# Rotary embedding of the first two pairs summed inside TensorE

## The chip, the cores and the metric

The kernel runs on one core of a Trainium2 chip. The core has TensorE (PE; its weight loads are listed apart as PEld), VectorE (DVE), ScalarE (ACT), GpSimd (POOL) and SyncE (SP, which issues most DMAs). PE reads SBUF and writes PSUM; the other engines move data between the two. The metric is the device time of one execution in microseconds (us), where less is better.

## What is computed

For 4 batches of 8 heads, 576 positions and head size 64, `q` and `k` are rotated (rotary embedding), softmax attention is taken, and the result goes through a mixer over positions and one over channels. In the reference:

```python
def rotate(x):
    x1, x2 = (x[..., :half], x[..., half:])
    return np.concatenate([x1 * cos - x2 * sin, x1 * sin + x2 * cos], axis=-1)
q_rot, k_rot = (rotate(q), rotate(k))
scores = scale * np.matmul(q_rot, k_rot.transpose(0, 1, 3, 2))
attn = softmax(scores); x = attn @ v
...
u = x + mix_over_positions(x);  out = u + relu(u @ w_ch1) @ w_ch2
```

## The kernel before

The 32 heads are worked on as 16 *pairs* (two heads of one batch, `n` = 0 to 15). The 576 positions are laid out as four rows `r` of 128 partitions and a fifth row of 64, kept in both partition halves, so a pair's `q` or `k` is a tile of 128 partitions x 5 rows x 2 heads x 64.

`prep(n)` loads `k`, `q` and `v` of a pair (`kraw`, `qraw`, `vraw`) and rotates `k` and `q` in three elementwise operations: `w = x * sin` (L486), `u = x * cos` (L488), and `u = u + w` with the two 32-wide halves of `w` exchanged (L492). Then TensorE transposes `u` in blocks of 64 partitions x 128 columns (L522, one instruction for each row `r` and partition half `z`), and ACT or DVE copies the result from PSUM to `kt` and `qt` (L540). For pair 0 the work is cut into rows 0 to 1 and rows 2 to 4, so that it starts before everything is loaded; I call these k part 1, k part 2 and so on. There is one `uk`, one `uq` and there are two `w` tiles, so pair 1 must wait for these tiles.

`pair(n)` makes scores (L666, 64 rows x 128 columns of weights, 288 columns moving; L584 for the fifth rows), scales them and takes the maximum on DVE (L551), the exponential on ACT (L563), transposes the probabilities on TensorE (L692, L608), copies them (L702), multiplies by `v` (L715), and normalizes (L744 and after). `warm` (L425) issues plain products with the identity into unused PSUM columns at the start, in which TensorE has nothing else to do. After the attention come the position mixer (L910, L932) and the channel mixer (L1001 to L1056).

All of it is fp32. A product that the code writes once is two pairs of records in the trace, a load of weights (LDWEIGHTS) and a product (MATMUL) each; a transpose is one pair. Blocks of 64 partitions use one half of TensorE's rows, so two of them (`z` = 0 and 1) can be under way at once.

What runs in which order is written out in two tables of numbers, `ORDER1` (1666 tasks, the attention and the first batch's position mixer) and `ORDER2` (195 tasks, the other position mixers and transposes). Each number is a task times four plus the chosen engine. PSUM banks are given out in this order too. Every engine then works through its own list in order. The later part of the channel mixer is ordered by the planner `Plan.run`.

Of the kernel before, what the change touches and what calls it, by code (L numbers as in the profile page):

```python
# [13 lines left out]
ALU = mybir.AluOpType  # L14
# [72 lines left out]
class Plan:  # L87
# [259 lines left out]
def rope_attention_mixer_kernel(ctx: ExitStack, tc: tile.TileContext, q, k, v, w_tok1, w_tok2, w_ch1, w_ch2, tab, out):  # L347
# [8 lines left out]
    nc = tc.nc  # L356
# [29 lines left out]
    def attention(ctx):  # L386
# [50 lines left out]
        def none(deps, bufs):  # L437
            return add("DVE", 0.0, None, deps, bufs)
# [5 lines left out]
        def prep(n):  # L444
# [3 lines left out]
            for nm, src, pr in (("k", k, 0.0), ("q", q, 0.5), ("v", v, 1.0)):  # L448
# [51 lines left out]
                for r0, r1 in parts:  # L500
                    if r0:
                        x = x + l[1:]
# [650 lines left out]
```

## Time and profile before

| what | us |
|---|---|
| three runs, median (lowest to highest) | 592.54 (592.42 to 592.59) |
| the profiled execution | 592.55 |
| its span, first to last instruction | 590.8 |
| PE busy in the span | 584.0 |
| DVE, ACT, POOL busy | 382.9, 312.9, 297.9 |

The profile lists the busy time of each engine, the share that it is of the span, and the chain of work that ended last: from the last instruction back to what released it, step by step. A busy PE isn't PE at its peak, since records of products contain a fixed latency and overlap; the pace is read from the distance between the starts of many like instructions. The granted clock of TensorE is full in the records of all stretches.

### The profile page before, as it was taken

How to read it: one execution, taken by the hardware profiler on the slowest of the kernel's cores; microseconds unless marked ns; L12 is line 12 of the kernel's file. 1: busy time of each engine (PE TensorE's matmuls, PEld its weight loads, DVE VectorE, ACT ScalarE, POOL GpSimd, SP SyncE). 2: the span in 40 equal slices, each digit the busy share in tenths (PEclk: the TensorE clock that was granted, in tenths of full speed). 3: DMA queues.
4: the chain of work that ended last, by engine and by line, in shares of the span. 5: the costliest groups of instructions: out<-in, count | busy, mean ns of one | idle time of the engine just before them, and what ended most of it. 6: DMA issues, size and time to landing. Idle time of an engine off the chain costs nothing.

```text
span 590.8 us, 12857 instructions
## 1 busy us (share of the span) xinstructions
PE 584.0 (99%) x4897; PEld 463.1 (78%) x4897; DVE 382.9 (65%) x1123; ACT 312.9 (53%) x797; POOL 297.9 (50%) x255
## 2 busy tenths in 40 slices
PE   8999999999999999999999999999999999999997
PEld 7767677777777676787888888888888888888886
DVE  6999989989999996789776543345423443222332
ACT  4999999999999998454444431333203311010110
POOL 4998498869779332323766761477404750000000
PEclk9999999999999999999999999999999999999999
DMA  5444122234141101022222220222102100001123
GB/s 141 140 133 131 33 69 68 74 79 147 38 141 27 32 1 55 7 85 72 53 63 68 64 75 1 70 65 53 28 0 72 37 1 0 1 0 72 71 72 107
DMA packets 34094, 36.15 MB, mean 61 GB/s; under 512 B 13809, under 2 KB 27633, under 8 KB 34033
## 3 DMA queue, kind: packets, MB, share of 16 engines
q1 hardware_dynamic: 32640, 34.81, 20.3%
q8 instruction: 38, 0.62, 0.4%
q10 hardware_dynamic: 1392, 0.52, 0.3%
q14 instruction: 24, 0.19, 0.1%
HBM read 30.61 MB, written 4.72 MB: 60 GB/s over the span
## 4 chain that ended last, share of the span: by engine, by line
PE 97%; DVE 2%; DMA 1%; ACT 0%; issue 0%; POOL 0%; DVEq 0%
PE s L1027 25%; PE s L1054 25%; PE s L715 14%; PE s L666 11%; PE s L692 7%; PE s L932 5%; PE s L910 4%; PE s L522 2%; PE s L584 2%; PE s L608 1%; PE s L1001 1%; PE s L744 1%; DVE p L551 1%; DMA tabs<-in_tab_dram 1%; DVE uq L492 0%
## 5 line engine op out<-in xcount | busy, mean ns | idle before, releaser
L1029 ACT ACTIVATE gh<-s 128x512 fp32r<-128x512 f32 (+1 forms) x60 | 33.3, 556 | 178.5 <-PE s L1027 178.5
L563 ACT ACTIVATE p<-p,nm 128x576 f32<-128x576 f32 x128 | 98.9, 778 | 2.5 <-DVE p L551 2.1
L1031 DVE SCALAR_TENSOR_TENSOR gl<-s,gh 128x512 fp32r<-128x512 f32 (+1 forms) x60 | 38.3, 638 | 95.2 <-ACT gh L1029 95.2
L1027 PE MATMUL s<-uh,c1h 128*128 128x512 f32 (+1 forms) x240 | 88.6, 369 | 0.0
L1027 PE MATMUL s<-ul,c1h 128*128 128x512 f32 (+1 forms) x240 | 88.3, 368 | 0.0
L1027 PE MATMUL s<-uh,c1l 128*128 128x512 f32 (+1 forms) x240 | 88.3, 368 | 0.0
L1056 DVE TENSOR_TENSOR X<-s,X 128x512 f32<-128x512 f32 (+1 forms) x65 | 44.4, 684 | 67.7 <-PE s L1054 67.5
L1054 PE MATMUL s<-c2l,gh 128*128 128x512 f32 (+1 forms) x219 | 84.6, 386 | 0.0
L1054 PE MATMUL s<-c2h,gh 128*128 128x512 f32 (+1 forms) x219 | 84.6, 386 | 0.0
L1054 PE MATMUL s<-c2h,gl 128*128 128x512 f32 (+1 forms) x219 | 84.5, 386 | 0.0
L715 PE MATMUL s<-pt,vraw 128*64 128x256 f32 (+1 forms) x640 | 84.5, 411 | 0.0
L666 PE MATMUL s<-kt,qt 64*128 64x288 f32 x512 | 78.1, 419 | 0.3 <-ACT kt L540 0.3
L715 PEld LDWEIGHTS s<-pt,vraw 128*64 128x64 f32 x640 | 43.7, 136 | 29.6 <-DVE p L551 1.3
L702 ACT COPY pt<-s 128x256 f32<-128x256 f32 (+1 forms) x167 | 59.6, 408 | 6.3 <-PE s L692 5.0
L551 DVE TENSOR_SCALAR_CACHE_REDUCE p<-s,nm 128x288 f32<-128x288 f32 x128 | 61.7, 512 | 1.8
L812 POOL TENSOR_TENSOR fa<-fc,fa 128x512 f32<-128x512 f32 (+3 forms) x31 | 34.8, 1123 | 52.2 <-DVE fa L810 27.3
L692 PEld LDWEIGHTS s<-ident,p 64*128 64x128 f32 x1152 | 46.1, 139 | 15.9 <-ACT p L563 3.9
L551 DVE TENSOR_SCALAR_CACHE_REDUCE p<-s 128x288 f32<-128x288 f32 x128 | 54.4, 452 | 2.5 <-PE s L666 1.8
L666 PEld LDWEIGHTS s<-kt,qt 64*128 64x128 f32 x512 | 49.9, 187 | 6.8 <-DVE p L551 0.9
L692 PE MATMUL s<-ident,p 64*128 64x64 f32 x1152 | 51.6, 226 | 0.3
L1027 PEld LDWEIGHTS s<-uh,c1h 128*128 128x128 f32 x240 | 45.2, 188 | 7.7
L1027 PEld LDWEIGHTS s<-ul,c1h 128*128 128x128 f32 x240 | 45.2, 188 | 7.6
(117 smaller groups left out, 1062.7 us busy)
## 6 DMA issues: line engine op xcount, KB each, us to landing
stg<-in_moe_w_ch_dram SPq DMA_DIRECT2D x16, 384.0 KB, 3.2
stg<-in_moe_w_ch_dram SPq DMA_DIRECT2D x12, 512.0 KB, 3.6
vraw<-in_v_dram SPq DMA_DIRECT2D x16, 256.0 KB, 3.0
kraw<-in_k_dram SPq DMA_DIRECT2D x15, 256.0 KB, 3.3
qraw<-in_q_dram SPq DMA_DIRECT2D x15, 256.0 KB, 3.4
out_dram<-X SPq DMA_DIRECT2D x15, 256.0 KB, 2.3
stg<-in_moe_w_tok_dram SPq DMA_DIRECT2D x4, 512.0 KB, 4.2
kraw<-in_k_dram SPq DMA_DIRECT2D x32, 32.0 KB, 2.6
```

The lines of the kernel that those rows point to most:

```text
L551: return lambda: nc.vector.tensor_scalar(out=p()[:, c * W2:(c + 1) * W2], in0=sb.t[:, 0:W2], scalar1=-D ** -0.5, scalar2=nm.t[:, 0:1] if c ...
L563: return lambda: nc.scalar.activation(out=p(), in_=p(), func=ACTF.Exp, bias=nm.t[:, 1:2], scale=-1.0, accum_out=l())
L666: nc.tensor.matmul(sbs[h].t[:, c0:c0 + W2], flat(qt.t)[halves[h], TL + j * P:TL + (j + 1) * P], flat(kt.t)[halves[h], TL * (1 - h) + u * W ...
L692: nc.tensor.transpose(xy[z].t[:, i * TL:(i + 1) * TL], pb.t[halves[z], c0:c0 + P], ident[halves[z], halves[z]])
L702: return lambda: e(out=pt[c].t[:, R * h:R * h + m, o + z * TL:o + (z + 1) * TL], in_=xy[z].t[:, 0:m * TL].rearrange("p (r s) -> p r s", r=m))
L715: nc.tensor.matmul(ab.t[halves[h], 0:w], vb.t[:, h, r, :], m, start=(r == 0), stop=(r == R))
L812: mul_ = lambda e: lambda: e.tensor_tensor(out=A(), in0=C(), in1=A(), op=ALU.mult)
L1027: nc.tensor.matmul(tb.t[:, 0:n], a, m, start=(i == 0), stop=(i == len(lst) - 1))
L1029: x = add("ACT", act(n), lambda f=f, tb=tb: nc.scalar.activation(out=gb.t[0][:, f, 0:n], in_=tb.t[:, 0:n], func=ACTF.Relu), [x], [tb, gb], ...
L1031: y = add("DVE", dve(n), lambda f=f, tb=tb: nc.vector.scalar_tensor_tensor(out=gb.t[1][:, f, 0:n], in0=tb.t[:, 0:n], scalar=0.0, in1=gb.t[ ...
L1054: nc.tensor.matmul(tb.t[:, 0:w], a, m, start=(i == 0), stop=(i == len(lst) - 1))
L1056: y = add("DVE", dve(w) + 0.08, lambda u=u, tb=tb, cols=cols, w=w: nc.vector.tensor_tensor(out=u[:, cols], in0=tb.t[:, 0:w], in1=u[:, cols ...
```

## The change

For the first two pairs (`n < ADDED`, with `ADDED = 2`) the third elementwise operation, the addition, is left out. The first operation writes `w` with its two halves already exchanged. In place of one transpose of `u`, TensorE makes two plain products with the identity into the same PSUM place, one of `u` and one of `w`, the second added to the first. The two elementwise operations no longer stand one behind the other (each waits for the load alone), and `w` is held until TensorE has read it. Pairs 2 to 15 are as before. Both order tables are new throughout.

```diff
 ORDER1 = (
-    72, 68, 80, 84, 88, 92, 96, 104, 100, 0, 12, 16, 21, 24, 4, 28, 32, 8, 40, 44, 48, 52, 76, 60, 108, 112, 152, 156, 148, 184, 56, 161, 36, 64, 1408,
...
+        ADDED = 2
...
-                        if i == 0:
+                        if i == 0 and n < ADDED:
+                            turn = lambda x: x.rearrange("p r h (a j) -> p r h a j", a=2)
+                            e.tensor_tensor(out=turn(w)[:, :, :, ::-1], in0=turn(src), in1=turn(bc(1)), op=ALU.mult)
+                        elif i == 0:
                             e.tensor_tensor(out=w, in0=src, in1=bc(1), op=ALU.mult)
...
+                    x0, xs = x, []
                     for i in range(3):
                         w = (r1 - r0) * 2 * D
+                        if n < ADDED and i == 2:
+                            none([], [])
+                            x = xs
+                            continue
+                        if n < ADDED:
+                            x = x0
...
                         for i in range(r1 - r0):
                             for z in range(2):
                                 r = (i - 1) % (R + 1) if z and first else r0 + i
-                                nc.tensor.transpose(xy[z].t[:, i * TL:(i + 1) * TL],
-                                                    ub.t[halves[z], r].rearrange("p h d -> p (h d)"), ident[halves[z], halves[z]])
+                                to, flat_ = xy[z].t[:, i * TL:(i + 1) * TL], lambda b: b.t[halves[z], r].rearrange("p h d -> p (h d)")
+                                if n < ADDED:
+                                    for b in (ub, wb):
+                                        nc.tensor.matmul(to, flat_(b), ident[halves[z], halves[z]], start=b is ub, stop=b is wb)
+                                else:
+                                    nc.tensor.transpose(to, flat_(ub), ident[halves[z], halves[z]])
...
-                    t = add("PE", 0.06 * (r1 - r0) + 0.012, tr, x, [*xy, ub, tb], pp, mode="row")
+                    added = n < ADDED
+                    t = add("PE", (0.25 if added else 0.06) * (r1 - r0) + 0.012, tr, x, [*xy, ub, tb] + [wb] * added, pp, mode="row")
```

Lines below the change are 17 higher in the changed file: L551 there is L568, L666 is L683, L692 is L709; the rotation's products are L537.

DVE, from the start of the program, before (`w_108`, `uq_107` and `qraw_101` are of q, `w_109`, `uk_106` and `kraw_99` of k; 256 columns are part 1, 384 part 2, 640 all of pair 1):

```order
L486 TENSOR_TENSOR w_108<-qraw_101,tabs 128x256
L488 TENSOR_TENSOR uq_107<-qraw_101,tabs 128x256
L492 TENSOR_TENSOR uq_107<-uq_107,w_108 128x256
L486 TENSOR_TENSOR w_109<-kraw_99,tabs 128x256
L492 TENSOR_TENSOR uk_106<-uk_106,w_109 128x256
L486 TENSOR_TENSOR w_109<-kraw_99,tabs 128x384
L488 TENSOR_TENSOR uk_106<-kraw_99,tabs 128x384
L492 TENSOR_TENSOR uk_106<-uk_106,w_109 128x384
L486 TENSOR_TENSOR w_108<-qraw_101,tabs 128x384
L488 TENSOR_TENSOR uq_107<-qraw_101,tabs 128x384
L486 TENSOR_TENSOR w_109<-kraw_100,tabs 128x640
L492 TENSOR_TENSOR uq_107<-uq_107,w_108 128x384
```

The same place on DVE now:

```order
L488 TENSOR_TENSOR w_108<-qraw_101,tabs 128x4x2x32
L492 TENSOR_TENSOR uk_106<-kraw_99,tabs 128x256
L492 TENSOR_TENSOR uk_106<-kraw_99,tabs 128x384
L488 TENSOR_TENSOR w_109<-kraw_99,tabs 128x6x2x32
L492 TENSOR_TENSOR uq_107<-qraw_101,tabs 128x384
L557 COPY kt_110<-s 128x2x64
L488 TENSOR_TENSOR w_108<-qraw_101,tabs 128x6x2x32
L568 TENSOR_SCALAR p_116,nm_139<-s 128x288
L568 TENSOR_SCALAR p_116,nm_139<-s,nm_139 128x288
```

Six products and one copy now stand ahead of the first maximum, where twelve operations stood, and DVE works on pair 1's rotation no more.

POOL, after its memsets, before (pair 1's `uk`, `w` and `uq`, the addition of k, then pair 2):

```order
L488 TENSOR_TENSOR uk_106<-kraw_99,tabs 128x256
L488 TENSOR_TENSOR uk_106<-kraw_100,tabs 128x640
L486 TENSOR_TENSOR w_108<-qraw_102,tabs 128x640
L488 TENSOR_TENSOR uq_107<-qraw_102,tabs 128x640
L492 TENSOR_TENSOR uk_106<-uk_106,w_109 128x640
L486 TENSOR_TENSOR w_109<-kraw_99,tabs 128x640
```

The same place on POOL now:

```order
L492 TENSOR_TENSOR uq_107<-qraw_101,tabs 128x256
L488 TENSOR_TENSOR w_109<-kraw_99,tabs 128x4x2x32
L488 TENSOR_TENSOR w_109<-qraw_102,tabs 128x10x2x32
L492 TENSOR_TENSOR uk_106<-kraw_100,tabs 128x640
L488 TENSOR_TENSOR w_108<-kraw_100,tabs 128x10x2x32
L492 TENSOR_TENSOR uq_107<-qraw_102,tabs 128x640
L490 TENSOR_TENSOR w_108<-kraw_99,tabs 128x640
```

POOL now makes all four products of pair 1, and its first operation for pair 2 (the last row) writes a `w` that TensorE reads before.

PE, from the middle of pair 0's scores to pair 1's rotation, before (`p_116` and so on are probabilities; the next rows are L584 and then pair 1's scores):

```order
L666 MATMUL s<-kt_110,qt_113 128x288 x4
L692 MATMUL s<-ident,p_116 128x64 x10
L666 MATMUL s<-kt_110,qt_113 128x288 x2
L692 MATMUL s<-ident,p_117 128x64 x18
L522 MATMUL s<-ident,uk_106 128x64 x10
L522 MATMUL s<-ident,uq_107 128x64 x10
L692 MATMUL s<-ident,p_118 128x64 x18
```

The same place on PE now, down to the first rows of pair 1's k:

```order
L683 MATMUL s<-kt_110,qt_113 128x288 x4
L709 MATMUL s<-ident,p_116 128x64 x10
L683 MATMUL s<-kt_110,qt_113 128x288 x4
L537 MATMUL s<-ident,uk_106 128x64
L537 MATMUL s<-ident,w_108 128x64
L537 MATMUL s<-ident,uk_106 128x64
L537 MATMUL s<-ident,w_108 128x64
```

The pattern of `u` and `w` goes on for 20 rows of k and then 20 of q (each a product in the code, for 10 transposes before); then come 18 transposes of `p_117`, 18 of `p_119` with the fifth rows' scores between them, and pair 1's scores.

## Rows read from the trace of the kernel before

**Rows 1.** The page's busy times and its chain by engine

```profile
PE 584.0 (99%) x4897; PEld 463.1 (78%) x4897; DVE 382.9 (65%) x1123; ACT 312.9 (53%) x797; POOL 297.9 (50%) x255
...
PE 97%; DVE 2%; DMA 1%; ACT 0%; issue 0%; POOL 0%; DVEq 0%
```

**Rows 2.** Chain of waits, first 24 us: start us, us, what

```profile
7.67 0.57 DVE uk L492
...
8.28 0.42 PE s L522 x6
...
8.72 0.67 ACT kt L540 x3
...
9.43 1.31 PE s L666 x8
...
11.96 2.68 DVE p L551 x14
...
16.46 0.94 DVE uq L492
...
20.05 2.14 PE s L666 x16
```

**Rows 3.** PE's groups from 9.42 to 19.9 us: count | busy, mean ns

```profile
L666 PE MATMUL s<-kt,qt 64*128 64x288 f32 x32 | 5.4, 425 | 0.3 <-ACT kt L540 0.3
L692 PE MATMUL s<-ident,p 64*128 64x64 f32 x54 | 3.7, 234 | 0.3
L584 PE MATMUL s<-kt,qt 64*64 64x288 f32 x16 | 1.2, 415 | 0.0
L522 PE MATMUL s<-ident,uq 64*128 64x64 f32 x16 | 1.0, 227 | 0.3 <-DVE uq L492 0.3
L522 PE MATMUL s<-ident,uk 64*128 64x64 f32 x10 | 0.5, 232 | 0.1
```

**Rows 4.** Chain of waits, whole span: dense stretches of PE

```profile
108.52 1.17 PE s L692 x36
...
119.43 2.00 PE s L666 x16
...
148.21 1.17 PE s L584 x16
```

**Rows 5.** Instructions in order of time: start us, us, engine, what [idle before]

```profile
3.55 2.06 SPq L458 DMA_DIRECT2D kraw<-in_k_dram  x3
...
5.51 0.73 POOL L488 TENSOR_TENSOR uk<-kraw,tabs 128x256 f32<-128x256 f32 x1 [2.65 <-DVE w L486]
...
6.61 0.55 DVE L486 TENSOR_TENSOR w<-kraw,tabs 128x384 f32<-128x384 f32 x1
...
7.08 0.55 DVE L488 TENSOR_TENSOR uk<-kraw,tabs 128x384 f32<-128x384 f32 x1
...
9.12 0.82 DVE L486 TENSOR_TENSOR w<-kraw,tabs 128x640 f32<-128x640 f32 x1
...
10.63 1.55 POOL L488 TENSOR_TENSOR uk<-kraw,tabs 128x640 f32<-128x640 f32 x1 [4.39 <-DMA vraw<-in_v_dram]
...
16.37 1.01 DVE L492 TENSOR_TENSOR uq<-uq,w 128x640 f32<-128x640 f32 x1
```

**Rows 6.** Instructions of PE alone, 4.8 to 5.9 us: the warming products

```profile
4.58 1.50 PE L425 MATMUL s<-ident 64*128 64x128 f32 x24
```

**Rows 7.** Instructions of three lines: count, duration ns min/median/max, first and last start

```profile
L425 PEld LDWEIGHTS s<-ident x72: 188/188/335, 1.3 to 8.8; 64*128 64x128 f32 x72
L425 PE MATMUL s<-ident x72: 271/272/580, 1.3 to 8.9; 64*128 64x128 f32 x72
...
L692 PEld LDWEIGHTS s<-ident,p x1152: 134/139/143, 12.6 to 233.1; 64*128 64x128 f32 x192
...
L584 PEld LDWEIGHTS s<-kt,qt x128: 129/133/133, 18.8 to 202.3; 64*64 64x64 f32 x128
```

**Rows 8.** DMA issues of the first 25 us: count, KB each, median us to landing

```profile
kraw<-in_k_dram SPq DMA_DIRECT2D x9, 32.0 KB, 2.7
```

More of the change, by code (lines that the diff above doesn't have):

```diff
@@ L512, in prep @@
                                  for z0, z1 in ((0, R + 1),)]
+                        xs = xs + x
                     one, xy = duo() if n else (None, [Buf(banks), Buf(banks)])
@@ L516, in prep, with tr @@
                     first = int(n > 0)
-                    def tr(r0=r0, r1=r1, xy=xy, ub=ub, first=first, nm=nm):
+                    def tr(r0=r0, r1=r1, xy=xy, ub=ub, wb=wb, first=first, nm=nm):
                         for i in range(r1 - r0):
```

147 rows, old and new, of tables (ORDER1, ORDER2) are left out of this document.

## The prediction

> **What bounds the kernel now.** I read the page's chain first: 97% of it is PE, and DVE has only 2% [rows 1]. So whatever makes PE's list longer anywhere makes the kernel longer, and help for another engine counts only where PE waits. Where that is, the chain of the first 24 us tells [rows 2]. Up to 20.05 us it runs over DVE (additions and products of the rotation, then maxima), ACT's copies and PE by turns. From the scores of pair 1 at 20.05 us on it is PE to the end: 590.8 - 20.05 = 570.75 us, 96.6% of the span, which is the PE share. So the change can win only ahead of 20.05 us, and I ask how much later or earlier pair 1's scores start.
>
> Next comes how much waiting there is to win. From the first scores (9.43 us) to 20.05 us are 10.62 us, and PE's records in that stretch are 32 of scores, 54 transposes of probabilities, 16 of the fifth rows' scores and 16 + 10 transposes of the rotation [rows 3]. Their pace is read from dense stretches [rows 4]: 36 transposes took 1.17 us, 0.0325 each; 16 records of scores 2.00 us, 0.125 each; the 16 of the fifth rows 1.17 us. The work is 32 x 0.125 + (54 + 26) x 0.0325 + 1.17 = 4.00 + 2.60 + 1.17 = 7.77 us. PE therefore waited 10.62 - 7.77 = 2.85 us there, mostly for maxima on DVE (2.68 us of the chain in one piece) and for the addition of pair 1's q (0.94 us) [rows 2].
>
> **Part 1, what leaves DVE and POOL.** Four additions of pair 0 (k part 2's took 0.57 us) and one of pair 1 (1.01 us) leave DVE, and pair 1's product of 0.82 us goes to POOL [rows 2, 5]. DVE spends about 3 us on the rotation (four products of 384 columns at 0.55, two of 256 at some 0.4 by the same measure) in place of about 7 (five of 256, six of 384, and the 0.82 and 1.01). POOL keeps as much: two short products of 0.73 us and four of 1.55, an addition less and a product more. Writing `w` with exchanged halves I cost at nothing: reading it exchanged (L492) took as long as a straight product at 384 columns, 0.57 against 0.55 [rows 2, 5].
>
> **Part 2, what PE gets.** Thirteen rows of rotation stand after the first scores: three of pair 0's q part 2 and ten of pair 1. Each had two transposes and now has four products in the code, eight records, four on each half of the array. The trace has no plain product of 64 moving columns with 64 x 128 weights. Two rows bound its pace.
>
> From below: the transposes, with the same operands, go at 0.0325 a record, 0.065 for two on both halves [rows 4]. From above: the warming products have the same weights, plain, with 128 columns moving. 24 of them start in 1.50 us; without the last one's own 0.27 us [rows 7] these are 11 steps of two, 0.112 each [rows 6]. Which is nearer? That depends on whether the product or the load sets the pace. A record of a load has a median of 188 ns for the warming products, 139 for transposes of the same 64 x 128 block, and 133 for the fifth rows, plain but with half the columns [rows 7]. So 64 columns of plain load are 55 ns, 128 are 110, and a transpose loads its 128 in half of that. 110 ns is the warming products' step. The product itself would be short: 2.00 us / 8 steps x 64/288 = 0.056. With half the moving columns the load stays as it is, so I take 0.112 a step.
>
> A row is then 4 x 0.112 = 0.446 us, where it was 0.065; thirteen rows cost 5.80 us in place of 26 x 0.0325 = 0.85, **4.95 us more**.
>
> **Part 3, when the first scores start.** Before, k part 2 needed three operations on DVE, the last ending at 8.24, and its six transposes, 0.20 us, ended at 8.48; copies, then scores at 9.43 [rows 2]. Now two operations are enough. They need the second tail of k, whose load is the first of the three issued from 3.55 us [rows 5] and is still the fifth in its queue; such a load takes 2.7 us [rows 8], so 6.3 is the start (before, DVE came to it at 6.61, behind its own work). Then 0.47 us from start to start (6.61 to 7.08) and 0.55 for the last make 7.3, 0.9 us earlier [rows 5]. But PE must first do k part 1, two rows or 0.89 us. Its `w` comes from POOL (0.73 us, behind POOL's own first product) at about 6.2, so PE is through at 7.2, and with two warming products at 7.4. Three rows of k part 2, 1.34 us, end at 8.75: 0.27 later than before. One of the three copies behind it moves from ACT to DVE, which gives back about 0.2. First scores: 9.5.
>
> **Part 4, the sum.** From 9.5 us PE has 4.00 + 54 x 0.0325 + 1.17 + 5.80 = 12.7 us of work. Does anything else hold it up? DVE is free at about 9.7 and has 16 maxima of at most 0.52, 8 us; PE needs the last ones after 20 us. POOL starts pair 1 behind DVE's last product at 9.8 and has k's two tiles three operations later, 14.4, and q's at 16; PE comes to k at about 15.4 and to q at 17.6. The copies of q into place lie beside 26 transposes (0.85 us). So no wait is left that I can name: pair 1's scores start at 9.5 + 12.7 = 22.2, **2.2 us later** than at 20.05. Behind that PE has the same work as before, and before it didn't wait there, so nothing is given back: 592.55 + 2.2 = **594.7** for an execution like the profiled one, which lies at the median of the runs. In short, 2.85 us of waits are filled up by 4.95 us of new work.
>
> One wait is new behind this point: POOL's first product for pair 2 writes a `w` that PE reads until pair 1's k is through, about 17.6; queued behind it are the other five operations of pair 2. Five at 1.5 us bring pair 2's k at about 25.3. PE wants it after pair 1's scores (2.0), a product with `v` (2.3) and some 2 us of transposes and scores, at 28.7 by the paces of [rows 4]. 3.4 us cover it; without the cover PE would wait in full.
>
> For this forecast by itself 593.9 to 595.8: the start of the scores may be 9.2 or 9.8, the step 0.110, and up to 0.6 us of small waits may remain.
>
> **Rivals.** *The load hides and the pace is that of transposes* (not slower). If a plain load of 128 columns can be spread so that a step takes 0.065, a row is 0.26 and thirteen are 3.4 us. Scores start at 8.9, and 8.9 + 4.00 + 1.76 + 1.17 + 3.4 = 19.2, to which DVE's maxima and copies add some half of a microsecond: 0.2 to 0.8 us earlier than before, 591.7 to 592.4. The turning point is a step of about 0.07. For it speaks that the product is short; against it the 188 ns of every plain load of 128 columns.
>
> *No load behind a product on the same half.* The two products of a block stand one behind the other on one half of the array. If the load of the second waited for the product of the first, a step would be 0.11 + 0.056 = 0.167 and a row 0.67: 2.9 us more in the thirteen rows, 1.1 more in the five of k before the scores, 598.7. The warming products speak against it: there a half's next load overlaps with its product, or the step would be over 0.2 [rows 6]. [...]
>
> *The new order loses elsewhere*, by the wait on `w` or by others after 20 us: 0.5 to 2 us on top, 595.3 to 597. That it wins elsewhere is excluded within what the chain shows, since PE never gives way there.
>
> **How the numbers follow.** Forecast 0.57, cheap loads 0.24, no overlap 0.12, loss elsewhere 0.07. The predicted time is 594.7. The range goes from 592.0 to 598.0: it takes in more than half of the cheap loads' case, and leaves out its lower part and nearly all of the no-overlap case, some 0.2. About 0.2% (1.2 us) is what a measurement can tell from no change, so "same" is 591.4 to 593.7. Faster: the best third of cheap loads, 0.09. Same: the rest of that, 0.15, and the lower edge of the forecast, 0.05. Slower: 0.71.
>
> **What would show it.** In the changed profile the load records of the rotation's products (L537) should be about 188 ns, not 139; the five rows of pair 1's k, and of its q, should take 2.2 us each, with scores first at 9.5 and pair 1's at 22.2, and PE alone in the chain from there. Five rows in 1.3 us, with pair 1's scores ahead of 20, would make the prediction wrong towards faster; five rows in 3.3 us towards slower.

## The result, and the profile after

| | median (lowest to highest) | runs |
|---|---|---|
| before | 592.52 us (592.42 to 592.95) | 6 |
| after | 596.21 us (595.45 to 596.87) | 6 |

The ratio is 1.0062 (95%: 1.0049 to 1.0075), so the change costs 3.7 us. The forecast was 594.7: right in sign, inside the range that was to hold it (592.0 to 598.0), outside the forecast's own range (593.9 to 595.8). The traced execution is the one of 596.87, with a span of 595.1; 2.2 us of its 4.3 had been forecast.

The page's busy times and its chain by engine, against [rows 1]:

```profile
PE 590.0 (99%) x5017; PEld 469.4 (79%) x5017; DVE 383.0 (64%) x1119; ACT 311.8 (52%) x794; POOL 300.3 (50%) x256
...
PE 98%; ACT 1%; DVE 0%; POOL 0%; issue 0%; POOLq 0%; ACTq 0%
```

PE has 120 pairs of records more (20 rows of the rotation, eight pairs in place of two), 6.0 us more busy time, and DVE's 2% of the chain are gone. The chain of waits from the start, against [rows 2] (start us, us, what):

```profile
1.34 6.46 PE s L425 x60
7.80 1.84 PE s L537 x32
9.64 0.23 PE s L425 x4
9.86 1.34 PE s L537 x22
11.20 0.50 PE s L425 x8
11.70 1.58 PE s L683 x12
13.28 1.23 PE s L537 x22
14.51 0.59 PE s L683 x4
15.10 0.30 PE s L709 x7
15.40 1.15 PE s L683 x8
16.55 0.31 PE s L709 x10
16.86 1.03 PE s L683 x8
17.89 4.46 PE s L537 x80
22.35 0.87 PE s L709 x25
23.22 1.13 PE s L601 x16
24.35 0.45 PE s L709 x10
24.80 2.00 PE s L683 x16
```

Read it from the top: PE is the chain from its first warming product at 1.34 us on, without a gap. L683 is the scores: the first at 11.70 (before 9.43, forecast 9.5), pair 1's at 24.80 (before 20.05, forecast 22.2). Where PE doesn't wait, the chain counts a group from the end of the record before it; by its own start the first group of scores begins 0.2 us earlier (PE's instructions in order of time):

```profile
11.50 0.86 PE L683 MATMUL s<-kt,qt 64*128 64x288 f32 x4
```

Behind pair 1's scores nothing changed: 595.1 - 24.80 = 570.3 us, before 570.75. The traces of all experiments below but *split32* have 570.3 to 571.4 there too, so pair 1's scores tell what a kernel gains or loses.

The rotation's products (L537), against [rows 7] (count, duration ns min/median/max, first and last start):

```profile
L537 PEld LDWEIGHTS s<-ident,w x80: 188/188/188, 7.8 to 22.1; 64*128 64x128 f32 x80
L537 PE MATMUL s<-ident,w x80: 272/272/272, 7.8 to 22.1; 64*128 64x64 f32 x80
```

These are the warming products' own durations, as forecast, and ten rows of pair 1 took 4.46 us, 0.446 a row: the forecast to the digit. So the price was right and the start was wrong, and the first question is why the first scores came 2.2 us after 9.5.

### The profile page after: what moved, and what is told of

It reads as the page before. It is cut to its first block, busy times and chain, and to the rows that moved or that the text cites. A ratio compares the mean times of both kernels' runs of the same rounds, so it can differ in the third digit from the quotient of the medians.

```text
span 595.1 us, 13088 instructions
## 1 busy us (share of the span) xinstructions
PE 590.0 (99%) x5017; PEld 469.4 (79%) x5017; DVE 383.0 (64%) x1119; ACT 311.8 (52%) x794; POOL 300.3 (50%) x256
## 4 chain that ended last, share of the span: by engine, by line
PE 98%; ACT 1%; DVE 0%; POOL 0%; issue 0%; POOLq 0%; ACTq 0%
PE s L1044 25%; PE s L1071 25%; PE s L732 13%; PE s L683 11%; PE s L709 7%; PE s L949 5%; PE s L927 4%; PE s L601 2%; PE s L537 1%; PE s L539 1%; PE s L425 1%; PE s L1018 1%; PE s L625 1%; PE s L761 1%; ACT p L580 0%; DVE p L568 0%
## 5 line engine op out<-in xcount | busy, mean ns | idle before, releaser
L683 PE MATMUL s<-kt,qt 64*128 64x288 f32 x512 | 76.9, 419 | 0.0
L829 POOL TENSOR_TENSOR fa<-fc,fa 128x512 f32<-128x512 f32 (+2 forms) x32 | 36.6, 1143 | 59.2 <-DVE fa L827 17.9
L568 DVE TENSOR_SCALAR_CACHE_REDUCE p<-s,nm 128x288 f32<-128x288 f32 x128 | 61.8, 513 | 2.5 <-PE s L683 0.6
L719 ACT COPY pt<-s 128x320 f32<-128x320 f32 (+1 forms) x159 | 56.4, 407 | 6.1 <-PE s L709 5.3
L709 PEld LDWEIGHTS s<-ident,p 64*128 64x128 f32 x1152 | 44.6, 139 | 17.1 <-ACT p L580 4.9
L568 DVE TENSOR_SCALAR_CACHE_REDUCE p<-s 128x288 f32<-128x288 f32 x128 | 54.3, 453 | 1.6 <-PE s L683 0.6
L683 PEld LDWEIGHTS s<-kt,qt 64*128 64x128 f32 x512 | 48.6, 188 | 7.0 <-ACT pt L719 0.9
L1044 PEld LDWEIGHTS s<-uh,c1l 128*128 128x128 f32 x240 | 45.2, 188 | 7.5
```

What stands on the lines that cost most here:

```text
L568: return lambda: nc.vector.tensor_scalar(out=p()[:, c * W2:(c + 1) * W2], in0=sb.t[:, 0:W2], scalar1=-D ** -0.5, scalar2=nm.t[:, 0:1] if c ...
L683: nc.tensor.matmul(sbs[h].t[:, c0:c0 + W2], flat(qt.t)[halves[h], TL + j * P:TL + (j + 1) * P], flat(kt.t)[halves[h], TL * (1 - h) + u * W ...
L709: nc.tensor.transpose(xy[z].t[:, i * TL:(i + 1) * TL], pb.t[halves[z], c0:c0 + P], ident[halves[z], halves[z]])
L719: return lambda: e(out=pt[c].t[:, R * h:R * h + m, o + z * TL:o + (z + 1) * TL], in_=xy[z].t[:, 0:m * TL].rearrange("p (r s) -> p r s", r=m))
L829: mul_ = lambda e: lambda: e.tensor_tensor(out=A(), in0=C(), in1=A(), op=ALU.mult)
L1044: nc.tensor.matmul(tb.t[:, 0:n], a, m, start=(i == 0), stop=(i == len(lst) - 1))
```

## The experiments

In each `before` ran on the same chip beside the others (medians of 592.5 to 592.6 us). The two columns on the right are from the one traced execution, which for most kernels is among the longer ones (599.69 for *price_only*, 594.41 for *before_warm22*, 598.24 for *warm8*, but 595.29 for *bridge*).

| run | median (lowest to highest), us | ratio to before | first scores | pair 1's scores |
|---|---|---|---|---|
| after_again | 596.63 (595.98 to 597.03) | 1.0064 (1.0051 to 1.0077) | 11.79 | 24.89 |
| price_only | 598.45 (597.83 to 599.69) | 1.0101 (1.0089 to 1.0113) | 12.05 | 26.55 |
| no_price | 592.06 (591.54 to 593.73) | 0.9992 (0.9984 to 1.0001) | 8.47 | 19.44 |
| old_order | 598.67 (598.04 to 598.85) | 1.0100 (1.0087 to 1.0113) | 11.79 | 26.29 |
| order_only | 596.44 (596.10 to 597.45) | 1.0071 (1.0059 to 1.0084) | 9.66 | 24.85 |
| k0_only | 594.08 (593.05 to 594.58) | 1.0022 (1.0013 to 1.0031) | 11.19 | 21.69 |
| warm22 | 597.69 (597.18 to 598.48) | 1.0089 (1.0075 to 1.0102) | 12.38 | 25.48 |
| before_warm22 | 593.67 (593.21 to 594.41) | 1.0018 (1.0009 to 1.0027) | 9.71 | 21.42 |
| warm8 | 594.96 (594.89 to 598.30) | 1.0058 (1.0036 to 1.0079) | 11.41 | 26.11 |
| bridge | 597.98 (595.02 to 600.73) | 1.0098 (1.0064 to 1.0133) | 9.98 | 23.08 |
| alternate | 596.07 (595.52 to 596.79) | 1.0053 (1.0034 to 1.0073) | 11.53 | 24.63 |
| split32 | 616.69 (one run) | | | |

**When does PE's queue begin to bind?** *after_again* is the change unaltered.

> The changed kernel once more, unaltered, for a second trace of it. Theory L (TensorE's list is the bound from its first product on): the first scores start 4.06 us after the warming products end, and these end when TensorE's pace has doubled early (4.3 us, as in the trace of before: end at 6.2 us) or late (7.3 us, as in the first trace of after: 7.64 us). So first scores at 10.3 to 11.7, pair 1's scores 13.1 us later, and the time of the profiled execution 595.4 to 596.9, later by as much as the pace doubled later. Rival D (data bound the start: loads, POOL and DVE beside each other): first scores at 11.5 or later, wherever the pace doubles.

It repeats the first trace: first scores at 11.79, 13.1 us on to pair 1's. That is 0.1 us behind theory L's late case and fits rival D as well, so it doesn't decide between them; *warm22* and *bridge* below do. The reason for the late start shows in the warming products. Their durations in the change's first trace, then in before's, there in two stretches:

```profile
L425 PE MATMUL s<-ident x54: 414/418/578, 1.3 to 7.1; 64*128 64x128 f32 x54
```

```profile
L425 PE MATMUL s<-ident x26: 417/418/580, 1.3 to 4.1; 64*128 64x128 f32 x26
```

```profile
L425 PE MATMUL s<-ident x36: 271/272/418, 4.1 to 6.1; 64*128 64x128 f32 x36
```

Before, the products fell from 418 to 272 ns (0.213 to 0.112 us from step to step) at 4.4 us; after, at 7.3. So the same 60 records end at 7.6 us where they ended at 6.2, and the rotation stands behind them in PE's list. The column of the granted clock reads 1.00 in both stretches, but for the slow products the trace holds no record of the clock at all: the first one, of full clock, starts at 4.43 us in before and at 7.33 in after. In each of the 14 traces of this case it starts where the products become short, so I take the doubling for the clock's. The pace ahead of it is near that of a granted 0.50: in *warm8* below a stretch at 0.50 has steps of about 0.2 again (20 records of the rotation in 2.03 us).

The moment lies anywhere from 4.19 us (*split32*) to 7.55 (*price_only*), and PE's list doesn't set it: after, *alternate* and *split32* begin with the same 60 records, and their full clock starts at 7.33, 7.19 and 4.19. Both traces of after are late ones (7.33 and 7.51). No trace of it with an early doubling was had, so that its faster executions (595.45 the fastest) are the early ones is argued and not shown.

*warm22* puts 14 more of these products ahead of the rotation, *before_warm22* does so before:

```diff
-        warm(15)
+        warm(22)
```

> The changed kernel with 44 warming products in place of 30 ahead of the first rotation. Theory L (TensorE's list sets the end from its first product on): 14 more steps of two records, 0.112 us each at the full pace, 7 x 2 x 0.112 = 1.57 us more, all of it in the time: 597.6 to 598.3 where the changed kernel has 596.1 to 596.6; executions in which the pace doubles late pay the same, unless it doubles after the first 30. Rival D (data bound the start): 596.0 to 596.8, no change.

> The same for the kernel before, 44 warming products in place of 30. There the first scores waited for the rotation on DVE (ended 8.24 us), and the 30 products ended at 6.2 us in the trace. With 44 they end at 7.8 (pace doubled early) to 9.1 us (late), so by theory L between 0 and 1.0 us is lost, 592.5 to 593.5, clearly less than the 1.57 us of the changed kernel: what stands ahead of the rotation was free before and is not any more.

The change pays 1.1 to 1.5 us of the added 1.57 (597.69 against 596.2 to 596.6), so the queue of PE binds its start and not the data. In *warm22* the pace doubled at 5.5 us:

```profile
1.34 7.14 PE s L425 x88
8.48 1.84 PE s L537 x32
...
12.38 1.58 PE s L683 x12
```

Its warming products end at 8.3 us, and from there to the first scores it is 4.06 us, as in the first trace of after from 7.64 to 11.70. The other half of the test didn't tell the two apart: before pays 1.1 us too, where I had put 1.0 at most. Its trace, of the longest execution (594.41), has the first scores only 0.28 us later than before's and the transposes of probabilities ahead of pair 1's scores (L692) 0.19 later; then the clock falls (windows: PE, its loads, DVE, ACT, POOL busy; the granted clock):

```profile
10.00:18.20 8.20, 7.71 (x95) 6.26 (x94) 8.13 (x35) 6.97 (x22) 6.73 (x5) 1.00 0.60 162
...
19.30:21.40 2.10, 2.10 (x18) 0.77 (x18) 0.84 (x4) 2.07 (x7) 2.10 (x2) 0.50 0.67 200
```

The fifth rows' scores (L584) took 2.13 us there, where before has 1.13. So before has a reserve under its warming products, as the 0.28 shows, and the traced execution lost most by the fall of the clock. The other ten (593.21 to 593.97) hardly did: their mean granted clock is 0.999 to 1.000, where the traced one has 0.997. They are 0.7 to 1.4 us longer than before all the same. A late doubling would explain up to 1.0 of it, as I had expected; the rest stays open.

*warm8* takes 14 of the 30 products away, *bridge* puts 6 of them back between q part 1 and k part 1:

```diff
-        warm(15)
+        warm(8)
...
+                        if n == 0 and nm == "q" and not r0:
+                            warm(3)
```

> The changed kernel with 16 warming products in place of 30 at the start. Theory L: the warming products end at 4.8 us, so the queue of TensorE waits for data instead; q part 1 starts at about 5.0, k part 1 at 6.8 (its w from POOL ends at 6.71), k part 2 at about 8.0 to 8.4, first scores at 9.8 (pace doubled by 4.3 us) to 10.2 (by 7.3 us). That is 0.4 to 1.5 us less than the changed kernel with the pace doubled at the same time: 594.7 to 595.4. Rival C (fewer products before keep the pace low for longer): half pace until 9 us or later, first scores at 11 to 12, 596 to 597. Rival D: no change, 596.2.

> The changed kernel with 16 warming products at the start in place of 30, and 6 more between the products of q part 1 and those of k part 1, where TensorE stood idle from 5.8 to 6.7 us with 16 alone and its granted clock fell to 0.50 in the traced execution. Theory L and the clock: no execution at 598 any more, all of them 594.7 to 595.8, by when the pace doubles; granted clock 1.00 from 7.6 to 14.4 us. Rival C2 (the fall has nothing to do with the idle time): some executions again at 598.

Four executions of *warm8* took 594.89 to 594.98, as theory L had it, and two 598.24 and 598.30. The trace is of a long one (columns as above):

```profile
4.80:6.70 1.90, 1.49 (x18) 1.21 (x18) 0.86 (x2) 0.80 (x1) 0.72 (x1) 1.00 0.85 238
...
7.60:14.40 6.80, 6.80 (x53) 6.23 (x52) 2.77 (x10) 1.47 (x6) 2.26 (x2) 0.50 0.53 143
```

PE stood idle for 0.41 us while it waited for k part 1's `w` from POOL, and from 7.6 to 14.4 us its clock was at 0.50. My mend for that failed: in *bridge* PE goes on without a gap, in the traced execution at least, and still three executions at 600.6 to 600.7 beside three at 595.0 to 595.4. The traced one is of the short kind, with first scores at 9.98, so data doesn't hold the change at 11.70. The long ones are not of *warm8*'s kind: their mean granted clock is 0.999, where both long executions of *warm8* have 0.994. A doubling that comes later still would fit, since no clock is recorded ahead of it, but no trace shows it. So L's arithmetic holds in the short executions of both; what makes three of *bridge* 5.3 us longer stays open.

**What the products cost, and what they relieve.** *price_only* is the kernel before with the new price and no relief; *no_price* is the change with transposes of `u` alone, so the part of the rotation that is in `w` is left out for pairs 0 and 1.

```diff
 price_only, on before
-                                nc.tensor.transpose(xy[z].t[:, i * TL:(i + 1) * TL],
-                                                    ub.t[halves[z], r].rearrange("p h d -> p (h d)"), ident[halves[z], halves[z]])
...
+                                if n < 2:
+                                    for _ in range(2):
+                                        nc.tensor.matmul(to, a, ident[halves[z], halves[z]], start=True, stop=True)
...
 no_price, on after
-                                    for b in (ub, wb):
-                                        nc.tensor.matmul(to, flat_(b), ident[halves[z], halves[z]], start=b is ub, stop=b is wb)
+                                    nc.tensor.transpose(to, flat_(ub), ident[halves[z], halves[z]])
```

> The kernel before, with its order and its additions on DVE and POOL, but each transpose of the rotated u of pairs 0 and 1 is made as two plain products with the identity into the same place (the second writes over the first). Theory L: TensorE's new work is as in the change (0.446 us a row in place of 0.065) with no relief: first scores at 10.3 to 11.4, pair 1's scores at 23 to 26, the time 595.2 to 598.3, I say 597. Rival O: the products fit into waits of 2.85 us and more, 592.5 to 593.7.

> The changed kernel, same order and same elementwise work, but TensorE only transposes u, as before; the product of w is left out, so half of the rotation of pairs 0 and 1 is not computed. Theory L: the work of TensorE is that of before, so the relief of DVE and POOL shows by itself: first scores at about 9.0, pair 1's scores at 17.3 to 18.3 (7.8 us of work and 0.5 to 1.5 of waits for maxima and POOL), the time 590 to 591, 5 to 6 us under the changed kernel. Rival O (the new order or the wait on w costs the time, not the products): pair 1's scores after 20, 594 to 596.

The products cost 6.0 us in the old list, and 4.2 to 4.6 in the new one (596.2 to 596.6 against 592.06). The change without its products, so the relief and the new order together, gains some 0.4 us on before, which the interval doesn't tell from nothing, where I expected 2. Its chain says why:

```profile
13.44 2.31 DMA kraw<-in_k_dram
...
15.79 0.69 POOL uq L492
...
16.53 0.52 PE s L536 x10
...
19.44 2.00 PE s L682 x16
```

Pair 1's `uq` now comes from POOL as the last of four products of 1.55 us, and is finished at 16.48, while PE stands idle (PE's instructions in order of time):

```profile
16.53 0.52 PE L536 MATMUL s<-ident,uq 64*128 64x64 f32 x10 [1.83 <-POOL uq L492]
```

Before, DVE's addition ended at 17.40 [rows 2]. DVE's wait was exchanged for POOL's, 1 us earlier, and 0.6 of that reached pair 1's scores. So even with products for nothing the change would have gained next to nothing.

**The order.** *old_order* has all edits and before's two tables; *order_only* has the new tables, the additions back behind their products, and transposes.

```diff
 order_only, on after; in ORDER1 each of the six additions stands behind the later of its two products
-        ADDED = 2
+        summed = lambda n, nm: n < 0
```

> All edits of the change but with both order tables of the kernel before. Theory L (TensorE's list is the bound from its first product on, whatever the order): the same 7 us of rotation products in the list, so 595.5 to 598, I say 596.8, between the changed kernel (596.5) and the kernel with the products alone and no relief (598.45). Rival O (the new order costs the time): 592.5 to 594.5.

> The new order tables without the sums on TensorE: the six additions are back, each right behind the two products that it needs, and TensorE transposes as before. In this order POOL has pair 1's four products of 1.55 us and k's addition, and DVE q's addition of 1.0 behind them: pair 1's q would be ready at about 19 us where it was at 17.4, so pair 1's scores at about 22 and the time 594 to 595 (the new order is made for the sums and is no gain by itself). Rival G (the order alone carries a gain): 592.2 or less.

Both came out longer than I had said. *old_order* equals *price_only*: in the old order the relief is worth nothing. Its chain between the first scores and pair 1's:

```profile
11.79 1.29 PE s L688 x8
13.08 1.23 PE s L542 x22
14.32 1.52 PE s L688 x11
...
16.24 1.61 DVE p L573 x8
...
19.81 4.63 PE s L542 x80
...
26.29 1.89 PE s L688 x13
```

The first scores come as late as in after (11.79), but PE then waits for maxima on DVE (L573) at 16.2, and 14.5 us go by where after takes 13.1. The new order fills that wait. By itself it is a loss (the chain, then windows as above):

```profile
17.36 1.55 POOL uq L496
...
18.93 0.84 DVE uq L500
...
24.85 2.27 PE s L686 x11
```

```profile
16.00:20.00 4.00, 0.85 (x16) 0.58 (x16) 2.03 (x8) 2.91 (x9) 3.06 (x3) 0.87 0.34 89
20.00:25.00 5.00, 5.00 (x64) 3.55 (x64) 4.54 (x17) 2.25 (x7) 5.00 (x4) 0.50 0.82 265
```

Pair 1's q is ready at 19.8, 0.8 us later than I had said; then PE, idle for most of 16 to 20 us, goes on at a granted 0.50. The records from 19.81 to 24.85, 46 transposes and the 16 of the fifth rows, would take 46 x 0.0325 + 1.17 = 2.7 us at the paces of [rows 4], an estimate; the other 2.4 are the clock's, which I had not counted on. No execution of *order_only* escaped such a fall, by its mean granted clock of 0.994 to 0.997. *no_price*, the same order without the additions, is 4.4 us shorter: relief and new order pay only together, and what they pay is the 0.4 us above.

**Part of the change alone.** *k0_only* is before with only pair 0's k summed on PE.

```diff
-        ADDED = 2
+        summed = lambda n, nm: n == 0 and nm == "k"     # and before's tables
```

> The kernel before, with its order, and only pair 0's k summed on TensorE (five rows, 2.2 us of products); pair 0's q and pair 1 keep their additions and transposes. DVE is relieved of 0.42 + 0.57 us ahead of the first scores. Theory L: TensorE's list reaches the first scores at 9.6 us (pace doubled early) to 10.9 (late), so no gain: 592.4 to 594, I say 593. Rival R (a few rows fit where TensorE waits, so that a part of the change pays): 591.3 to 592.2.

No gain, and 0.1 us more than I had allowed. The first scores come at 11.19, 0.3 behind my late case, in a trace whose pace doubled at 7.3 us.

**What sets the pace of a product.** *split32* makes each product as two of 32 moving columns; *alternate* issues u and w in turn on the two halves of the array.

```diff
 split32
-                                    for b in (ub, wb):
-                                        nc.tensor.matmul(to, flat_(b), ident[halves[z], halves[z]], start=b is ub, stop=b is wb)
+                                    for c in (0, TL // 2):
+                                        o = halves[z].start + c
+                                        for b in (ub, wb):
+                                            nc.tensor.matmul(to[:, c:c + TL // 2], flat_(b), ident[halves[z], o:o + TL // 2], start=b is ub, stop=b is wb)
 alternate
-                        for i in range(r1 - r0):
-                            for z in range(2):
+                        for i, b, z in itertools.product(range(r1 - r0), (ub, wb) if n < ADDED else (ub,), range(2)):
```

> The changed kernel with each of the rotation's products made as two of 32 moving columns with the same weights, 16 records a row in place of 8. If the load of the weights sets the pace (as the prediction took), the step stays 0.112 and a row of pair 1 takes 0.89 us, ten rows 8.9; the rotation costs 7.1 us more after pair 0's first rows and some 3 more before, 603 to 607. If the product sets it, the step halves and a row stays at 0.45, 596 to 597. If a fixed time per record sets it, the result is as with the load, but then the record of a load would be no longer than that of a transpose (139 ns), where it was 188.

> The changed kernel with the four products of a row in another order: u on one half of the array, u on the other, then w on both, so that no two products in a row stand on one half. If loads overlap with the product before them only when that is on the other half, the changed kernel would pay for its two products in a row on each half, and ten rows of pair 1 here would take less than the 4.46 us that they take in the changed kernel. By the prediction (the load alone sets the pace, 0.112 a step in either order) they take 4.46 us again, and the time is 595.5 to 597.0.

PE's instructions in order of time, in *split32*:

```profile
6.97 0.41 PE L539 MATMUL s<-ident,uq 64*128 64x32 f32 x4
7.20 0.41 PE L539 MATMUL s<-ident,w 64*128 64x32 f32 x4
7.45 0.41 PE L539 MATMUL s<-ident,uq 64*128 64x32 f32 x4
7.67 0.41 PE L539 MATMUL s<-ident,w 64*128 64x32 f32 x4
```

Each group of four records starts 0.22 to 0.25 us after the one before it; over 6.9 to 10 us that makes 0.118 a step of two with half the columns, where it was 0.112 with all. So the columns don't set the pace. Its loads last 188 ns as before, which speaks for the load; a fixed time per plain record isn't excluded by a run. The whole kernel took 616.69, 10 us above the upper end of what I had expected; its clock was at 0.50 in several stretches, the first from 11 us on, though PE had had no gap:

```profile
8.00:10.00 2.00, 2.00 (x37) 2.00 (x36) 0.56 (x1) 0.43 (x2) 0.00 (x0) 1.00 0.54 158
11.00:16.00 5.00, 5.00 (x48) 5.00 (x48) 0.17 (x1) 0.53 (x2) 0.00 (x0) 0.50 0.42 115
```

In *alternate* ten rows take 4.41 us (4.46 in the change), and the time is the same. It changes less than I had meant: a plain fp32 product is itself two records on one half, so on each half the records follow one another as in the change, and only the order between the halves is new.

```profile
17.82 4.41 PE s L536 x80
```

## Why the prediction was right in sign and too small

**What bounds** was right: all that was gained or lost lies ahead of pair 1's scores, and behind them nothing came back but 0.45 us.

**Part 2, the price,** was right: 0.446 a row, by the length of the records most likely set by the load. *Cheap loads* fell with it. *No load behind a product on the same half* fell too: after has two products in a row on each half, four records. If each load waited for the product before it, the step would grow with the moving columns; it is 0.118 with 32, 0.112 with 64 and 0.112 with the warming products' 128 [rows 6].

**Part 3, the start of the first scores,** is the step that failed: 9.5 forecast, 11.70 in the trace. I took the end of the data (k part 1's `w` at 6.2; in the trace 5.99 + 0.72 = 6.71, still ahead of PE's list) and added k's five rows. But PE's list has q part 1's two rows, 0.89 us, in front of k's, and the 30 warming products in front of these. From the last of them to the first scores it is 4.06 us: 7.64 to 11.70. With the end that before's trace shows (6.2) that makes 10.3, 0.8 later than forecast. The other 1.4 us are the late doubling of PE's pace (7.3 in place of 4.4 us). I had one trace, took its moment for fixed, and didn't ask what it would cost elsewhere, since before has a reserve there: its first scores wait for DVE's last addition, which ends at 8.24 [rows 2].

**Part 1, the relief,** I costed by what leaves DVE, and that was right, but POOL got two products for its addition, not one as I wrote, and I didn't ask what the relief is worth by itself. With the new order it is some 0.4 us (*no_price*), since POOL's list becomes the wait; in the old order nothing (*old_order*).

**Part 4, the sum,** held but for 0.4 us: from first scores to pair 1's 13.1 us in place of 12.7, with no wait: scores took 4.35 (4.00), transposes of probabilities 1.93 (1.76), products 5.69 (5.80), the fifth rows 1.13 (1.17). In all 2.2 forecast + 2.2 (start) + 0.4 - 0.45 = 4.35 us, and 596.87 - 592.55 = 4.32 in the traced execution.

**The new order loses elsewhere** fell: with the sums it saves 2.0 to 2.5 us against the old one. It was the wrong question; that the order alone carries a loss and the edits alone a larger one only the two experiments showed. The wait on `w` came as forecast (POOL's first product for pair 2 starts at 20.30, when PE has read pair 1's k), and nobody waited for it.

## What to carry to other kernels

Where work is moved onto an engine, add up that engine's own list from its first instruction, filler ahead of it included: filler that is free as long as others are late becomes part of the path. Ask also what the relief is worth if the price were nothing; here a chain that passes from DVE to POOL shows it is next to nothing. And look at a start-up rate in several traces before counting on its moment.

## What the runs showed of the hardware

- A plain fp32 product's pace here doesn't grow with its moving columns from 32 to 128: a step of two loads of 64 x 128 with their products takes 0.112 us with 128 columns [rows 6], 0.112 with 64 (after, 80 records in 4.46 us) and 0.118 with 32 (*split32*). The loads' records are 188 ns long each time. Transposes of the same block go at 0.065 for two [rows 4].
- PE's pace doubled (0.213 to 0.112 us a step in before) between 4.19 us after the start (*split32*) and 7.55 (*price_only*) in 14 traces, 4.43 in before, 5.5 in *warm22* and 7.33 in after among them, though PE was busy without a gap from 1.34 us to there in all. The first record of the granted clock starts there; the column reads 1.00 ahead of it too, for want of a record. What sets the moment, with a spread of 3.4 us, no run shows.
- The granted clock fell to 0.50 early on in four traces: behind 0.41 us of idle time (*warm8*), behind 0.49 idle of 8.2 us (*before_warm22*), behind 3.15 idle of 4 us (*order_only*), and with no gap at all in a row of products of 32 columns (*split32*).
- DVE's product of 384 columns took 0.97 us beside one on POOL of 0.72 us, where one took 0.55 alone [rows 5]:

```profile
6.15 0.97 DVE L492 TENSOR_TENSOR uk<-kraw,tabs 128x384 f32<-128x384 f32 x1 [0.25 <-DMA kraw<-in_k_dram]
```

```profile
5.99 0.72 POOL L488 TENSOR_TENSOR w<-kraw,tabs 128x256 f32<-128x256 f32 x1 [1.10 <-DVE uk L492]
```
